# First transfers of a float32 attention and rational FFN kernel: the coefficients on ScalarE's queue, one more pair of words in the fixed order, a bias as a number

## The chip, the cores and the metric

One core of a Trainium2 chip runs the whole program. The metric is device time in microseconds, the median of several executions. TensorE (PE) multiplies and transposes; VectorE (DVE), ScalarE (ACT) and GpSimd (POOL) do the elementwise work; SyncE (SP) issues the transfers between device memory and the on-chip memory. Each engine works through its own instructions in the order of the program and waits on semaphores for the others. TensorE's granted clock has two levels, 2.4 GHz (shown as 1.00) and 1.2 GHz (0.50).

## What is computed

```python
# q, k, v: [8, 8, 576, 64]; p: [8, 8, 32, 64]; w_in: [512, 2048]; w_out: [2048, 512]
def sm_attn(qq, kk, vv):
    s = scale * qq @ kk.T
    e = exp(s - max(s)); return (e / (sum(e) + 1e-9)) @ vv
packed = sm_attn(p, k, v)             # 32 rows of each head
x = sm_attn(q, packed, packed)        # [4608, 512] when the heads are put side by side
h = x @ w_in
P = a[0] + a[1]*h + a[2]*h*h + a[3]*h*h*h
Q = 1 + |b[0]|*|h| + |b[1]|*h*h
out = (P / (Q + 1e-6)) @ w_out
```

q, k, v, p, a and b are float32 here; the two weight matrices come in as 64-bit words (float64), and the kernel turns them into float32 itself. a has four numbers, b has two.

## The kernel before, in words

The batches are bb = 0 to 7. For each, `attention(bb)` makes the packed rows (PPT) and the transposed second softmax (AH, for bb > 0 also its rounded remainder AL). `m_chunk` multiplies the packed rows with a chunk of w_in (M). A unit is one batch, one half x of its 576 rows and one chunk c of 256 of the 2048 hidden columns: 128 units. `hidden` multiplies M with AH into a PSUM bank h, and then runs the rational function: ACT makes |h| (tile U), h squared (sq) and a part of P (Y); POOL adds U and sq; ACT takes the logarithm of the sum, with the bias (1 + 1e-6) * S that stands in a tile `one` of one column, and then the exponential of its negative, back into bank h; DVE does the rest and gives g (tiles gh and gl). `acc_block` multiplies g with w_out into the banks acc, three units later. There are two banks h, two banks acc and two banks at (for everything else).

The first units run in plain float32 and want the weights in words turned early. `load_words` loads one pair of 128-row blocks of words (two transfers of 512 KB), `convert` turns one pair: on ACT a first and a second half (two ACTIVATE of 1024 columns), on DVE two operations of 1024 columns, and an integer addition on DVE or POOL.

`constants` makes what depends on a and b: abS (the coefficients scaled by S), and in the tile `root` a scaled square root of |b[1]|, in a chain of small DVE operations with a logarithm and an exponential on ACT in its middle. ACT then reads some of these numbers into registers (TENSOR_LOAD), and uses them as scales in the units. a and b are loaded by two transfers on SP's queue, with the same value for all 128 partitions (2 KB and 1 KB).

The order of work: every operation outside the set-up goes to `Planner`, which has prices for operations, transfers and signals between engines, tries thirty schedules, and keeps the one that it counts as the shortest; each engine then gets its instructions in that schedule's order. The transfers before `nc.pin()` (the list at line 1004) keep their order and come first on SP. SP waits for a transfer eight places earlier before it issues the next, since eight semaphores go round. Where the plan leaves PE idle for over 180 ns in the first 150 us, `idle` puts in multiplications by a tile of zeros of 96 columns into an open acc bank, here called fillers (line 290): they add nothing to the sums. Each fp32 multiplication of float32 data leaves two records in the trace, so a filler leaves two.

Of the kernel before, what the change touches and what calls it, by code (L numbers as in the profile page):

```python
# [13 lines left out]
F32 = mybir.dt.float32  # L14
# [5 lines left out]
AF = mybir.ActivationFunctionType  # L20
ALU = mybir.AluOpType
AX = mybir.AxisListType
PSUM = bass.MemoryType.PSUM

P = 128
# [4 lines left out]
S = 2.0**-40  # L30


class Planner:
# [8 lines left out]
    TRANSPOSE, F32 = (15, 0.734), (30, 1.62)  # L42
# [19 lines left out]
    SWITCH = 95  # L62
    SLACK = 60, 100, 150, 220, 300
    IN_FLIGHT = 8
    DMA_ISSUE, DMA_START, DMA_END = 420, 1400, 1200

    DMA_RATE = 100.0, 190.0, 370.0
# [27 lines left out]
    def cost(self, engine, name, args, kwargs):  # L95
        if engine == "sync":
            return self.DMA_ISSUE
        fixed, per = self.COST[engine]
        if engine == "tensor":
            if name == "transpose" or args[1].dtype == F32:  # L100
                fixed, per = self.TRANSPOSE if name == "transpose" else self.F32
        aps = [x for x in args if isinstance(x, bass.AP)]
        if engine == "scalar":
            fixed += (aps[-1].space == PSUM) * -42 + ("accum_out" in kwargs) * 93 + ("bias" in kwargs) * 93
            per += 0.1 * any(x.ap[-1][0] == 2 for x in aps[:2])
        if engine == "gpsimd" and len(aps) < 3:
            fixed, per = 135, 0.9
        if engine == "vector" and len(aps) > 2 and any(self.columns(x) == 1 for x in aps[1:]):
            fixed += 60
        if engine == "vector" and name == "tensor_scalar" and len(aps) == 2:  # L110
            per /= 2
        return fixed + per * self.columns(aps[1] if name.startswith("reduce") else aps[0])
# [45 lines left out]
    def edges(self):  # L158
# [32 lines left out]
            edges.append(before)  # L191
        return edges

    def schedule(self, before, after, rank, back=0):

        n = len(rank)
        need = [len(x) for x in before]
        at, start, end = [0.0] * n, [0.0] * n, [0.0] * n
        soon = {e: [] for e in self.ENGINES}
        ready = {e: [] for e in self.ENGINES}  # L200
        free = dict.fromkeys(self.ENGINES, 0.0) if back else dict(self.FIRST)
        port = {"vector": 0.0, "gpsimd": 0.0}
        mode, landed, dma = None, [], 0.0
        for i in range(n):
            if not need[i]:
                heapq.heappush(soon[self.ops[i][0]], (0.0, rank[i], i))
        now = 0.0
        left = n
        while left:
            for e in self.ENGINES:  # L210
                while soon[e] and soon[e][0][0] <= now:
                    heapq.heappush(ready[e], heapq.heappop(soon[e])[1:])
                if free[e] > now or not ready[e]:
                    continue
                if e == "sync" and not back and len(landed) >= self.IN_FLIGHT and landed[-self.IN_FLIGHT] > now:
                    free[e] = landed[-self.IN_FLIGHT]
                    continue
                _, i = heapq.heappop(ready[e])
                left -= 1
                s = now  # L220
                if e == "tensor" and not back and self.modes[i] != mode:
                    s += self.SWITCH
                    mode = self.modes[i]
                if not back and self.shared[i]:
                    s = max(s, port["vector" if e == "gpsimd" else "gpsimd"])
                    port[e] = s + self.costs[i]
                start[i] = s
                end[i] = free[e] = s + self.costs[i]
                if e == "sync":
                    if back:  # L230
                        dma = max(dma, end[i]) + self.transfers[i]
                        end[i] = dma + self.DMA_START + self.DMA_END - self.DMA_ISSUE
                    else:
                        dma = max(dma, s + self.DMA_START) + self.transfers[i]
                        end[i] = dma + self.DMA_END
                        landed.append(end[i])
                for j in after[i]:
                    need[j] -= 1
                    f = self.ops[j][0]
                    way = self.WAY.get((f, e) if back else (e, f), self.PASS)  # L240
                    way += back * (way > 0)
                    at[j] = max(at[j], end[i] + way)
                    if not need[j]:
                        heapq.heappush(soon[f], (at[j], rank[j], j))
            now = min(
                t
                for e in self.ENGINES
                for t in ([free[e]] if ready[e] else [max(soon[e][0][0], free[e])] if soon[e] else [1e12])
            )
        return start, end  # L250
# [74 lines left out]
def attention_rational_ffn(  # L325
# [38 lines left out]

    sb = ctx.enter_context(tc.tile_pool(name="sb", bufs=1))
    ps = ctx.enter_context(tc.tile_pool(name="ps", bufs=1, space=PSUM))
    tc.nc.scalar.preload_act_table_set("natural_log_exp_and_others")
    nc = Planner(tc.nc)


    ident = sb.tile([P, P], F32, name="ident")
    make_identity(tc.nc, ident)
    ab, abS, one, root = (sb.tile([P, n], F32, name=x) for n, x in ((8, "ab"), (7, "abS"), (1, "one"), (5, "root")))
    ab, eps, minus = ab[:, 0:6], ab[:, 6:7], ab[:, 7:8]
    zero = sb.tile([P, 32], F32R, name="zero")
    win = sb.tile([P, NCH, NCC, CF], F32, name="win")
    G = sb.tile([P, NFC, 2 * REM], F32, name="G")
# [25 lines left out]
    def constants():  # L403
        nc.gpsimd.memset(eps, 1e-9)
        nc.gpsimd.memset(minus, -SCALE)
        nc.vector.tensor_scalar(zero, ident[:, 0:32], 0.0, None, ALU.mult)
        nc.sync.dma_start(ab[:, 0:4], a.rearrange("(o n) -> o n", o=1).broadcast_to([P, 4]))
        nc.sync.dma_start(ab[:, 4:6], b.rearrange("(o n) -> o n", o=1).broadcast_to([P, 2]))
        nc.vector.tensor_scalar(abS[:, 0:6], ab, S, None, ALU.mult)
        nc.vector.scalar_tensor_tensor(abS[:, 4:6], abS[:, 4:6], -1.0, abS[:, 4:6], ALU.mult, ALU.max)  # L410
        nc.vector.memset(one, (1.0 + 1e-6) * S)

        m, e, p, r, i = (root[:, n : n + 1] for n in range(5))
        nc.vector.scalar_tensor_tensor(m, ab[:, 5:6], -1.0, ab[:, 5:6], ALU.mult, ALU.max)
        nc.vector.tensor_scalar(m, m, 2.0**-126, None, ALU.max)
        nc.vector.tensor_scalar(e.bitcast(I32), m.bitcast(I32), 23, None, ALU.logical_shift_right)
        nc.vector.tensor_scalar(e.bitcast(I32), e.bitcast(I32), 127, None, ALU.add)
        nc.vector.tensor_scalar(p.bitcast(I32), e.bitcast(I32), 1, 23, ALU.logical_shift_right, ALU.logical_shift_left)
        nc.vector.reciprocal(i, p)
        nc.vector.tensor_scalar(m, m, i, i, ALU.mult, ALU.mult)  # L420
        nc.scalar.activation(r, m, AF.Ln)
        nc.scalar.activation(r, r, AF.Exp, scale=0.5)
        nc.vector.reciprocal(i, r)
        nc.vector.scalar_tensor_tensor(r, m, i, r, ALU.mult, ALU.add)
        nc.vector.tensor_scalar(abS[:, 6:7], r, p, 0.5 * S**0.5, ALU.mult, ALU.mult)
        for i, reg in enumerate((reg_a3, reg_b0, reg_b1, reg_root)):
            nc.scalar.reg_load(reg, abS[0:1, 3 + i : 4 + i].bitcast(I32))
# [458 lines left out]
    def hidden(bb, x, c):  # L886
# [4 lines left out]
        U, V, Y = U_ring.next(), h_ring.next()[:, :, 0:HALF], Y_ring.next()  # L891
        U2 = U2_ring.next()
# [13 lines left out]
        nc.vector.scalar_tensor_tensor(Y, Y, a1, V, ALU.add, ALU.mult)  # L906
        nc.gpsimd.tensor_add(U, U, U2)
        yield
        nc.scalar.activation(U2, U, AF.Ln, bias=one)
        nc.scalar.activation(V, U2, AF.Exp, scale=-1.0)  # L910
        nc.vector.scalar_tensor_tensor(Y, Y, a0, V, ALU.add, ALU.mult)
        nc.vector.scalar_tensor_tensor(V, U, (1.0 + 1e-6) * S, V, ALU.add, ALU.mult)
# [88 lines left out]
        elif i == 1:  # L1001
            nc.sync.dma_start(ov, o)

    for what in ("k0", "k1", "r", "p", "qr", 2, "rv", "v0", "v1", 3, "q0", "q1", 4, 5):
        if isinstance(what, int):
            load_words(what)
        else:
            load(0, what)
    nc.pin()
    constants()  # L1010
    for _ in attention(0):
        pass
# [17 lines left out]
    for bb in range(1, B):  # L1030
        gen = attention(bb)
        at = [u for u in range(2 * UB * bb - 30, 2 * UB * bb - 3) if u not in mt]
# [89 lines left out]
```

## Time and profile before

| | us |
|---|---|
| median of 3 runs | 765.78 (765.69 to 766.87) |
| the profiled execution, its own time | 766.86 |
| its span, first to last instruction | 765.1 |
| PE busy | 737.9 (96%) |
| DVE busy | 656.0 (86%) |
| ACT busy | 619.1 (81%) |
| POOL busy | 467.4 (61%) |

The profile gives, for each engine, when each instruction ran, how long it took, and how long the engine sat idle before it and for whom. The profiled execution took 1.08 us longer than the median, and 1.76 us of its time lie outside the span.

### The profile page before, as it was taken

To read this page: it belongs to the slowest core of one execution; us is meant where nothing else is said; L and a number is where in the kernel's file an instruction comes from. 1 tells how busy PE (TensorE), PEld (TensorE's weight loads), DVE (VectorE), ACT (ScalarE), POOL (GpSimd) and SP (SyncE) were. 2 spreads that over 40 slices of the span, in tenths; PEclk is the share of its full clock that TensorE was granted. 3 is DMA by queue.
4 is the path that set the end of the run, shared out by engine and by line. 5 is a ranking of instruction groups with operands and counts; after the bars stand their busy time and mean duration, and the time that the engine had idled before them with its cause. 6 is when DMAs were issued, how large, how long until landed. Compare 5 with 4: busy or idle time off the path is not lost.

```text
span 765.1 us, 14505 instructions
## 1 busy us (share of the span) xinstructions
PE 737.9 (96%) x5358; PEld 569.2 (74%) x5358; DVE 656.0 (86%) x1050; ACT 619.1 (81%) x1074; POOL 467.4 (61%) x457
## 2 busy tenths in 40 slices
PE   3689999999999999999999999999999999999997
PEld 2455645678788887778788887778788887778886
DVE  2789999898988889998998789998998889988773
ACT  6689986898786888888786888888786887887882
POOL 0026556987685566856685565955685655866672
PEclk8679999999999999999999999999999999999999
DMA  9994650203801128024701119222801016000001
GB/s 253 292 371 129 164 135 0 83 26 50 120 1 56 43 32 126 10 84 55 112 1 57 36 24 126 25 84 32 116 14 56 27 24 83 1 28 1 29 1 41
DMA packets 156630, 56.38 MB, mean 74 GB/s; under 512 B 126864, under 2 KB 145808, under 8 KB 156560
## 3 DMA queue, kind: packets, MB, share of 16 engines
q1 hardware_dynamic: 156560, 55.46, 32.8%
q8 instruction: 42, 0.69, 0.4%
q14 instruction: 28, 0.23, 0.1%
HBM read 46.01 MB, written 9.44 MB: 72 GB/s over the span
## 4 chain that ended last, share of the span: by engine, by line
PE 89%; DMA 4%; ACT 2%; DVE 2%; POOL 1%; SPq 1%; issue 1%; DVEq 0%; POOLq 0%; ACTq 0%
PE acc L293 46%; PE h L293 28%; PE at L293 15%; DMA m<-in_moe_w_in_dram 2%; PE acc L290 1%; DMA pn<-in_p_dram 1%; DVE Y L293 1%; SPq L293 1%; DMA AH<-in_k_dram 1%; ACT sq L293 0%; ACT U L293 0%; POOL U L293 0%; POOL gl L293 0%; ACT h L293 0%; ACT Y L293 0%
## 5 line engine op out<-in xcount | busy, mean ns | idle before, releaser
L293 POOL TENSOR_TENSOR U<-U,sq 128x576 f32<-128x576 f32 x128 | 185.3, 1448 | 140.9 <-ACT sq L293 135.7
L293 DVE SCALAR_TENSOR_TENSOR Y<-Y,abS,h 128x576 f32<-128x576 f32 x256 | 205.7, 804 | 55.0 <-ACT h L293 52.9
L293 PE MATMUL acc<-w,gh 128*128 128x512 f32 x736 | 240.8, 407 | 0.5 <-ACT half L293 0.5
L293 PE MATMUL h<-AH,m 128*128 128x288 f32 x1024 | 195.6, 315 | 1.7 <-DVE AH L293 1.0
L293 PEld LDWEIGHTS h<-AH,m 128*128 128x128 f32 x1024 | 159.2, 189 | 30.8 <-DVE Y L293 7.5
L293 POOL TENSOR_TENSOR gl<-Y,gh 128x512 fp32r<-128x512 f32 x116 | 150.2, 1296 | 31.2 <-POOL G L293 13.5
L293 PEld LDWEIGHTS acc<-w,gh 128*128 128x128 f32 x736 | 133.9, 188 | 45.6 <-issue 16.4
L293 PE MATMUL acc<-w,gl 128*128 128x512 f32 x384 | 150.6, 412 | 0.0
L293 ACT ACTIVATE sq<-U,one 128x576 f32<-128x576 f32 x128 | 101.1, 790 | 34.9 <-POOL U L293 34.7
L293 ACT ACTIVATE U<-h 128x576 f32<-128x576 f32 x128 | 83.3, 651 | 40.3 <-PE h L293 39.6
L293 DVE TENSOR_TENSOR Y<-Y,h 128x576 f32<-128x576 f32 x128 | 95.3, 745 | 16.0 <-ACT Y L293 15.7
L293 ACT ACTIVATE h<-sq 128x576 f32<-128x576 f32 x128 | 84.8, 663 | 21.6 <-DVE Y L293 20.0
L293 PE MATMUL h<-AL,m 128*128 128x288 f32 x448 | 97.0, 296 | 0.0
L293 ACT ACTIVATE Y<-h,abS 128x576 f32<-128x576 f32 x128 | 96.5, 754 | 0.0
L293 DVE SCALAR_TENSOR_TENSOR h<-U,h 128x576 f32<-128x576 f32 x128 | 95.9, 749 | 0.0
L293 PEld LDWEIGHTS acc<-w,gl 128*128 128x128 f32 x384 | 71.8, 188 | 22.9 <-issue 10.2
L293 DVE SCALAR_TENSOR_TENSOR Y<-h,Y 128x576 f32<-128x576 f32 x116 | 87.0, 750 | 1.9
L293 ACT CAST gh<-Y 128x512 fp32r<-128x512 f32 x116 | 73.0, 629 | 14.8 <-DVE Y L293 10.1
L293 ACT ACTIVATE sq<-h 128x576 f32<-128x576 f32 x128 | 83.5, 653 | 0.0
L293 PE MATMUL acc<-half,gh 128*128 128x512 f32 x240 | 78.2, 409 | 0.2 <-ACT gh L293 0.2
L293 PEld LDWEIGHTS h<-AL,m 128*128 128x128 f32 x448 | 71.9, 188 | 2.0 <-issue 1.4
L293 PEld LDWEIGHTS acc<-half,gh 128*128 128x128 f32 x240 | 43.9, 188 | 13.5 <-issue 5.1
(145 smaller groups left out, 904.3 us busy)
## 6 DMA issues: line engine op xcount, KB each, us to landing
w<-in_moe_w_out_dram SPq DMA_DIRECT2D x16, 512.0 KB, 5.1
out_dram<-half SPq DMA_DIRECT2D x15, 512.0 KB, 3.0
nat<-in_k_dram SPq DMA_DIRECT2D x48, 144.0 KB, 4.3
nat<-in_q_dram SPq DMA_DIRECT2D x48, 144.0 KB, 4.4
nat<-in_v_dram SPq DMA_DIRECT2D x24, 256.0 KB, 3.3
m<-in_moe_w_in_dram SPq DMA_DIRECT2D x10, 512.0 KB, 8.9
w<-in_moe_w_in_dram SPq DMA_DIRECT2D x6, 512.0 KB, 8.2
nat<-in_k_dram SPq DMA_DIRECT2D x4, 512.0 KB, 7.1
```

The source lines that it names most:

```text
L290: getattr(self.nc.tensor, name)(*args, **kwargs)
L293: getattr(getattr(self.nc, engine), name)(*args, **kwargs)
```

## The change

Three things. The two transfers of a and b leave SP's queue and `constants`; they become the first two instructions of ScalarE, issued on ScalarE's own queue ahead of its table load. The planner no longer orders them; in their place it counts what reads `ab` as ready 4.5 us after the start (`LANDED`, `ready`). The list of fixed first transfers gets a sixth pair of words. The bias of the logarithm is given as a number instead of the tile `one`, whose memset falls away, and the planner's price takes its 93 ns for a bias only where the bias is a tile.

```diff
+    LANDED = 4500.0
-            fixed += (...) + ("bias" in kwargs) * 93
+            fixed += (...) + isinstance(kwargs.get("bias"), bass.AP) * 93
...
+    def ready(self, calls):
+        return self.LANDED * any(isinstance(x, bass.AP) and x.tensor.name == "ab" for _, args, _ in calls for x in args)
...
-                heapq.heappush(soon[self.ops[i][0]], (0.0, rank[i], i))
+                at[i] = 0.0 if back else self.ready(self.ops[i][1])
+                heapq.heappush(soon[self.ops[i][0]], (at[i], rank[i], i))
...
+    tc.nc.scalar.dma_start(ab[:, 0:4], a.rearrange("(o n) -> o n", o=1).broadcast_to([P, 4]))
+    tc.nc.scalar.dma_start(ab[:, 4:6], b.rearrange("(o n) -> o n", o=1).broadcast_to([P, 2]))
     tc.nc.scalar.preload_act_table_set("natural_log_exp_and_others")
...
-        nc.sync.dma_start(ab[:, 0:4], a.rearrange("(o n) -> o n", o=1).broadcast_to([P, 4]))
-        nc.sync.dma_start(ab[:, 4:6], b.rearrange("(o n) -> o n", o=1).broadcast_to([P, 2]))
-        nc.vector.memset(one, (1.0 + 1e-6) * S)
...
-        nc.scalar.activation(U2, U, AF.Ln, bias=one)
+        nc.scalar.activation(U2, U, AF.Ln, bias=(1.0 + 1e-6) * S)
...
-    for what in ("k0", "k1", "r", "p", "qr", 2, "rv", "v0", "v1", 3, "q0", "q1", 4, 5):
+    for what in ("k0", "k1", "r", "p", "qr", 2, "rv", "v0", "v1", 3, "q0", "q1", 4, 5, 6):
```

Since the planner plans anew, the order of all engines changes beyond the first 25 us. Three places are shown. In the names, the first number belongs to the buffer and the last counts the tiles; kx, AH, at, acc, h, m, gh are as above, and w and half hold words or weights.

The first is the start of ACT, before:

```order
L1118 UNCONDITIONAL_BRANCH
L367 ACT_TABLE_LOAD
L293 COPY kx0_1_87<-at0_1_91 128x512
```

after:

```order
L1123 UNCONDITIONAL_BRANCH
L375 DMA ab_61<-in_moe_a_dram 128x4
L376 DMA ab_61<-in_moe_b_dram 128x2
L377 ACT_TABLE_LOAD
L299 TENSOR_LOAD abS_62 x2
L299 ACTIVATE root_63<-root_63 128x1 x2
L299 TENSOR_LOAD abS_62
L299 COPY kx0_1_89<-at0_1_91 128x512
```

The chain of the constants with its register loads now stands ahead of ACT's first copy; before, it stood some thirty-five instructions later, among the copies of chunk 1.

The second is ACT from the first units' three operations to the copies of batch 1's transposes, before:

```order
L293 ACTIVATE Y1_2_139<-h1_2_138,abS_68 128x576
L293 ACTIVATE sq0_1_129<-U0_1_126,one_69 128x576
L293 COPY m1_7_134<-at0_21_147 128x256
L293 ACTIVATE h0_1_127<-sq0_1_129 128x2x288
L293 COPY m1_7_134<-at1_22_148 128x256
L293 ACTIVATE sq1_2_140<-U1_2_137,one_69 128x576
L293 COPY kx0_2_141<-at0_23_154 128x512
L293 COPY kx0_2_141<-at1_24_155 128x512
L293 ACTIVATE h1_2_138<-sq1_2_140 128x2x288
L293 COPY kx0_2_141<-at0_25_159 128x256
```

after:

```order
L299 ACTIVATE Y1_2_140<-h1_2_139,abS_62 128x576
L299 COPY m1_7_135<-at0_21_148 128x256
L299 COPY m1_7_135<-at1_22_149 128x256
L299 ACTIVATE w2_5_121<-w2_5_121 128x1024
L299 ACTIVATE sq0_1_130<-U0_1_127 128x576
L299 ACTIVATE sq1_2_141<-U1_2_138 128x576
L299 ACTIVATE h0_1_128<-sq0_1_130 128x2x288
L299 COPY kx0_2_142<-at0_23_155 128x512
L299 COPY kx0_2_142<-at1_24_156 128x512
L299 ACTIVATE h1_2_139<-sq1_2_141 128x2x288
L299 COPY kx0_2_142<-at0_25_160 128x256
```

A half of a pair of words and both logarithms now stand ahead of the copies of the transposes at_23 and at_24.

The third is PE where batch 1's packed rows wait for DVE, before:

```order
L293 MATMUL at0_35_195<-rv0_2_110,small_74 32x64
L290 MATMUL acc1_14_167<-half0_1_157,zero_71 32x96 x14
L293 MATMUL at1_34_194<-ident_62,small_74 128x128
L290 MATMUL acc1_14_167<-half0_1_157,zero_71 32x96 x2
L293 MATMUL h0_7_190<-AH0_3_114,m1_7_134 128x288 x4
```

after:

```order
L299 MATMUL at0_35_196<-rv0_2_112,small_75 32x64
L299 MATMUL acc0_13_167<-half1_2_179,gl1_2_182 128x512 x2
L299 MATMUL acc1_14_168<-half0_1_158,gh1_2_172 128x512 x2
L299 MATMUL acc1_14_168<-half1_2_179,gl1_2_182 128x512 x2
L299 MATMUL at1_34_195<-ident_67,small_75 128x128
```

Six multiplications of the units' sums, done earlier before, now stand where 14 fillers stood. In the whole program there are 41 fillers before and 11 after (one of them 256 columns wide).

## Rows read from the trace of the kernel before

**Rows 1.** The page: the span.

```profile
span 765.1 us, 14505 instructions
```

**Rows 2.** Stretches: from:to, length, busy us by engine, PEclk, DMA share, GB/s.

```profile
0.00:38.00 38.00, 20.12 (x261) 13.75 (x261) 20.28 (x52) 23.79 (x44) 1.12 (x10) 0.79 0.93 273
38.00:53.00 15.00, 11.62 (x55) 8.10 (x56) 13.24 (x24) 11.19 (x23) 3.04 (x3) 0.73 1.04 365
53.00:100.00 47.00, 47.00 (x367) 28.14 (x366) 43.43 (x75) 46.80 (x79) 25.85 (x14) 1.00 0.65 180
100.00:168.00 68.00, 67.12 (x380) 39.98 (x378) 63.47 (x100) 55.87 (x88) 51.42 (x43) 1.00 0.17 44
168.00:761.00 593.00, 592.06 (x4298) 479.20 (x4298) 515.10 (x804) 481.42 (x843) 385.94 (x390) 1.00 0.27 48
```

**Rows 3.** Stretches, fillers of line 290 alone: PE, PEld busy, PEclk, DMA, GB/s.

```profile
53.00:100.00 47.00, 6.24 (x62) 4.95 (x62) 1.00 0.65 180
100.00:168.00 68.00, 1.84 (x20) 1.62 (x20) 1.00 0.17 44
```

**Rows 4.** PE in order of time: start, us, operation, count [idle before, released by].

```profile
20.89 1.92 PE L293 MATMUL acc<-w,kx 128*32 128x64 f32 x60 [0.97 <-DMA w<-in_v_dram]
...
38.25 4.21 PE L293 MATMUL h<-AH,m 128*128 128x288 f32 x8 [0.96 <-DVE AH L293]
...
48.98 1.98 PE L293 MATMUL at<-ident,nat 128*128 128x128 f32 x8 [2.98 <-ACT m L293]
50.99 1.12 PE L293 MATMUL at<-ident,AH 128*128 128x128 f32 x4
...
52.33 1.28 PE L293 MATMUL acc<-w,gh 128*128 128x512 f32 x2
53.45 2.10 PE L293 MATMUL h<-AH,m 128*128 128x288 f32 x8
```

**Rows 5.** ACT in order of time.

```profile
5.95 0.58 ACT L293 COPY kx<-at 128x512 f32<-128x512 f32 x1 [3.93 <-PE at L293]
...
23.66 1.15 ACT L293 ACTIVATE m<-m 128x1024 f32<-128x1024 f32 x1 [4.28 <-DMA m<-in_moe_w_in_dram]
...
42.23 1.19 ACT L293 ACTIVATE w<-w 128x1024 f32<-128x1024 f32 x1 [3.60 <-DVE abS L293]
43.31 1.06 ACT L293 COPY kx<-at 128x512 f32<-128x512 f32 x2
44.47 0.65 ACT L293 ACTIVATE U<-h 128x576 f32<-128x576 f32 x1
...
47.85 0.81 ACT L293 ACTIVATE sq<-U,one 128x576 f32<-128x576 f32 x1
48.52 0.41 ACT L293 COPY m<-at 128x256 f32<-128x256 f32 x1
48.77 0.71 ACT L293 ACTIVATE h<-sq 128x576 f32<-128x576 f32 x1
49.36 0.43 ACT L293 COPY m<-at 128x256 f32<-128x256 f32 x1
```

**Rows 6.** DVE in order of time: the second half of AH.

```profile
41.71 0.77 DVE L293 STREAM_TRANSPOSE AH<-kx 128x576 f32<-128x576 f32 x1
```

**Rows 7.** Stretches around batch 1's transposes, columns as in rows 2.

```profile
48.00:52.00 4.00, 2.87 (x13) 2.15 (x14) 3.78 (x6) 3.94 (x9) 0.86 (x1) 0.68 1.06 371
52.00:56.00 4.00, 4.00 (x29) 2.37 (x27) 3.46 (x6) 3.94 (x6) 0.00 (x0) 0.89 1.04 394
```

**Rows 8.** Transfers: operation, count, KB each, median us to landing.

```profile
pn<-in_p_dram SPq DMA_DIRECT2D x8, 16.0 KB, 4.7
ab<-in_moe_b_dram SPq DMA_DIRECT2D x1, 1.0 KB, 10.4
ab<-in_moe_a_dram SPq DMA_DIRECT2D x1, 2.0 KB, 9.3
```

**Rows 9.** The tile root: operations, count: ns min/median/max, first and last start.

```profile
L293 DVE TENSOR_SCALAR root<-root x5: 141/146/267, 34.5 to 37.2; 128x1 int32<-128x1 int32 x3, 128x1 f32<-128x1 f32 x2
```

More of the change, by code (lines that the diff above doesn't have):

```diff
@@ L103, in cost @@
         if engine == "scalar":
-            fixed += (aps[-1].space == PSUM) * -42 + ("accum_out" in kwargs) * 93 + ("bias" in kwargs) * 93
+            fixed += (aps[-1].space == PSUM) * -42 + ("accum_out" in kwargs) * 93 + isinstance(kwargs.get("bias"), bass.AP) * 93
             per += 0.1 * any(x.ap[-1][0] == 2 for x in aps[:2])
@@ L366, in attention_rational_ffn @@
     ps = ctx.enter_context(tc.tile_pool(name="ps", bufs=1, space=PSUM))
+    ab, abS, root = (sb.tile([P, n], F32, name=x) for n, x in ((8, "ab"), (7, "abS"), (5, "root")))
+    ab, eps, minus = ab[:, 0:6], ab[:, 6:7], ab[:, 7:8]
+    tc.nc.scalar.dma_start(ab[:, 0:4], a.rearrange("(o n) -> o n", o=1).broadcast_to([P, 4]))
+    tc.nc.scalar.dma_start(ab[:, 4:6], b.rearrange("(o n) -> o n", o=1).broadcast_to([P, 2]))
     tc.nc.scalar.preload_act_table_set("natural_log_exp_and_others")
@@ L372, in attention_rational_ffn @@
     make_identity(tc.nc, ident)
-    ab, abS, one, root = (sb.tile([P, n], F32, name=x) for n, x in ((8, "ab"), (7, "abS"), (1, "one"), (5, "root")))
-    ab, eps, minus = ab[:, 0:6], ab[:, 6:7], ab[:, 7:8]
     zero = sb.tile([P, 32], F32R, name="zero")
```

## The prediction, made before the changed kernel was run

> **What bounds the kernel now.** The first view is the table of stretches [rows 2], read for which engine is full where, and after it the single engines in order of time. Up to 38 us nothing is full for long: the 16 DMA engines are 93% busy, and PE waits for landings, as for v at 20.89 us [rows 4]. From 38 to 53 us the clock is at its lower level for part of the time (mean 0.73) and PE, DVE and ACT wait for one another. From 53 us on PE is the bound: it idles 0.88 us up to 168 us, and 0.94 us in the 593 us after that. But up to 168 us not all of its work is needed: 82 records of fillers, two to a filler, take 6.24 + 1.84 = 8.08 us [rows 3], 0.197 us a filler. There DVE (106.90 of 115 us) and, up to 100 us, ACT (46.80 of 47 us) are nearly full as well, so the fillers mark where PE waited for them. After 168 us a saving on any engine but PE is worth nothing. So the question is how much earlier PE gets through the first 168 us.
>
> **The change, part by part.**
>
> *The bias.* The logarithm goes from 0.67 us (47.85 to 48.52) towards the 0.59 us that the exponential takes between starts (48.77 to 49.36) [rows 5]: 0.08 us, times 128 some 10 us of ACT. Some 120 of the units run after 100 us, where ACT is idle for 124 us and PE doesn't wait for it: nothing. Up to 100 us it is about eight, 0.6 us of ACT; I count it in the fillers' term, since both are the same relief.
>
> *The coefficients at the start.* ACT's first copy (5.95 us) now stands behind the chain of the constants, and that behind the landing of a and b. The chain is some seven DVE steps of 0.146 us [rows 9], two small ACT steps, three more DVE steps and a register load; with a signal between each I estimate 3.3 us. What lies behind: the copies, the first attention, the words. The cover: ACT is idle 4.28 us before 23.66 us [rows 5], and PE waited 0.97 us for v [rows 4]; and ACT itself waited 3.93 us for PE before the first copy, and the next copies also come as fast as PE makes them. So I estimate that the copies can be some 2.3 us late for nothing. That holds for a landing up to 5.95 + 2.3 - 3.3 = 4.9 us from the span's start. The trace shows no small transfer with an empty queue. The nearest rows are 4.7 us for 16 KB, and 9.3 and 10.4 us for a and b themselves, behind SP's backlog [rows 8]. Issued at about 1 us, these give landings at 5.7 and 10.3 us, so a loss of 0.8 or of 5.4 us; below, a loss of nothing. I take 0.2 us, since here only the first transfer of k is in front of them.
>
> The rows put a and b behind a backlog of SP's. The Trainium skill (DMA: Bandwidth & Descriptors, "Issuing engines are not separate DMA queues") says that transfers issued from several engines run on the same 16 DMA engines and interleave, and that it saves only the time to issue. By it the second queue is no faster path, but interleaving would let a and b pass the megabytes of k, and the loss would be 0 instead of 0.2 us; no row here shows two queues side by side.
>
> *The sixth pair.* 1 MB of words takes the place of a and b on SP, ahead of batch 1's k. At 273 to 365 GB/s [rows 2] that is 2.7 to 3.8 us later for what follows. Batch 1's transposes of k come, in the order of before, only after the 38.25 us group of PE. In the new order they come just before it. So I cost it at nothing, with a bound of 1 us if k is late. In return ACT turns this pair in the 3.60 us that it waited for abS, up to 42.23 us [rows 5]. A copy of batch 1 still may not start until DVE has made the second half of AH (41.71 + 0.77 = 42.48 us) [rows 6], as the two share the buffer kx; so ACT gains work done ahead, not an earlier unit.
>
> *Early loss, 38 to 57 us.* From that point I follow ACT in the new order by the old times. Two copies of 0.53 and a half pair of 1.08 us (both from 42.23 to 44.37) [rows 5] from 42.9 us on: the first unit's operations start at 45.05 instead of 44.47 us. Six of these take 47.85 - 44.47 = 3.38 us, to 48.43. Two chunk copies of 0.25 us: 48.93, and PE makes the transposes at_23 and at_24 at the same 48.95 us as before. But then ACT does a half pair (1.08), two logarithms (0.59 each) and an exponential (0.59) before it copies them, so the copies end at 52.3 and 52.85. PE goes on with the next transposes at 52.5 instead of 50.99 us [rows 4], with batch 1's scores at 54.4, and with the first sum (acc) at 55.5 instead of 52.33. Up to 55.5 us the old order had done the sum's first multiplication (1.1 us) and the second pair of units' first half (2.1 us), the new one instead the scores (0.7): 2.5 us behind. In the old trace the clock fell to its lower level after the idle stretch before 48.98 and rose inside 52 to 56 us (means 0.68 and 0.89) [rows 7], when PE had been busy for close to 4 us. With more idle time in between it should rise later, near 57 us: another 0.6 us or more. I take 3.1 us of loss on PE, with bounds of 1.0 (ACT is not held up) and 4.5 us (all of it cold).
>
> *Fillers.* 30 of 41 go: 30 x 0.197 = 5.9 us that PE doesn't spend. What replaces the largest group, 14 of them where batch 1's packed rows wait for DVE, is work: six multiplications of the sums. That is the early loss coming back. But where the inputs are later than the plan, idle time takes the place of fillers. Call these new waits w: between 0 and 5.9 us. DVE says that w isn't 0: it is 93% busy up to 168 us and has its 8.1 us of idle time for this, of which the early loss takes some. I take 1.0 us, near the lower end, by PE's 0.88 us of idle time in the same stretch, which shows that the old plan's gaps were met.
>
> *After 168 us.* The order changes, PE's work doesn't: 0, with bounds of half a microsecond either way by the 0.94 us of idle time.
>
> Sum: -5.9 + 3.1 + 0.2 + 1.0 = -1.6 us. The profiled execution took 766.86 us, 1.76 of it outside its span of 765.1 [rows 1], which I leave as they are; it would take 765.3; its 1.08 us over the median are not the kernel's, so the median goes from 765.78 to 764.2.
>
> **Rivals.**
> 1. *The relief is real and the early loss isn't.* ACT starts 42.9 us with one pair more turned than before; if the copies aren't behind the half pair by a whole microsecond, the loss is 1.0 and w near 0: -4.9 at the most, -4.3 us with 0.6 of waits: 761.5.
> 2. *DVE bounds it.* The constants leave DVE's full stretch, but otherwise its work is the same, and 93% of the time is spoken for. Then w = 2.6 us, and the fillers were only a picture of a wait: 765.8. PE's unbroken run after each filler speaks against it, ACT's full 53 to 100 us for it.
> 3. *Slower: fillers turn into idle time.* The early loss stays because the second and third pair of units come some 3 us later from ACT, and DVE gets them too late to give it back. It decides at w = 2.6 us (no gain), and at w = 4.1 us the kernel is slower by 0.2%. At w = 5 us: 768.2.
> 4. *a and b land late.* As in the old trace, after 9.3 us: 5.4 us lost, 769.4. It decides at a landing near 4.9 us; for it speaks that k's transfers are issued at the same time, against it that the backlog of old is not there yet. The interleaving of the page named above lowers its chance; I give it 0.06.
> 5. *The change does not do what it says*, as the number for a bias might be put into a tile again: then the order shown would still hold, and only some tenths of ACT's time go: inside the forecast.
>
> **How the numbers follow.** 0.2% (1.53 us) is about what a measurement of this kernel can tell from no change. The forecast has 0.42, and as it lies on that line, 0.22 of it is faster and 0.20 the same. Rival 1 has 0.22 (faster), rival 2 0.18 (same), rival 3 0.12 and rival 4 0.06 (slower). So faster 0.44, same 0.38, slower 0.18. Range: from 760.8 (rival 1 with no waits) to 767.6, which leaves out most of rivals 3 and 4 and little else.
>
> **What would show it.** In the profile after: ACT's first copy at 7 to 8.3 us and PE's v product still near 20.9 us (the start is free); no 3.6 us wait of ACT near 42 us; the first acc multiplication near 55.5 us; fillers of about 2 us; PE idle by 1 to 3 us between 57 and 168 us; and after that the same 593 us. A first copy past 9 us, or an acc multiplication at 52 us, or idle time over 4 us would prove a step wrong, and so would a change of more than 1 us behind 168 us.

## The result, and the profile after

The changed kernel takes 774.38 us (median of 4 runs, 773.47 to 775.44), the kernel before 766.33 us beside it: a ratio of 1.0095, with an interval of 1.0076 to 1.0114. It is slower by 0.95%, where 0.2% faster was forecast, and lies outside the range. The profiled execution took 774.68 us; its span is 7.8 us longer than that of [rows 1].

```profile
span 772.9 us, 14401 instructions
```

The same stretches as in [rows 2], with the same columns; the last is given twice, first as long as it was before:

```profile
0.00:38.00 38.00, 20.81 (x245) 15.49 (x245) 19.41 (x50) 21.14 (x40) 1.06 (x9) 1.00 0.92 294
38.00:53.00 15.00, 10.39 (x64) 6.80 (x64) 12.74 (x21) 12.65 (x23) 5.49 (x4) 0.74 0.88 281
53.00:100.00 47.00, 43.77 (x277) 25.36 (x278) 41.65 (x73) 41.60 (x73) 21.45 (x12) 0.90 0.54 168
100.00:168.00 68.00, 66.40 (x400) 39.41 (x399) 63.36 (x98) 56.90 (x94) 52.14 (x41) 1.00 0.26 59
168.00:761.00 593.00, 589.07 (x4281) 473.69 (x4280) 522.80 (x808) 475.05 (x848) 385.53 (x390) 1.00 0.26 48
168.00:769.00 601.00, 596.83 (x4314) 479.78 (x4312) 523.64 (x810) 476.17 (x849) 388.06 (x392) 1.00 0.26 47
```

The trace of this execution holds no clock record before 31 us, so the mean clock of 1.00 in its first stretch says nothing; in e13, a run with the same order told below, it is 0.82. PE was idle for 0.94 us of the 593 us behind 168 us; now it is 3.93 us, and DVE is busy for 522.80 instead of 515.10 us of them. From 53 to 168 us PE's idle time goes from 0.88 to 4.83 us. The fillers, which answer to [rows 3], are down from 8.08 to 2.49 us:

```profile
53.00:100.00 47.00, 1.20 (x10) 0.77 (x10) 0.90 0.54 168
100.00:168.00 68.00, 1.29 (x11) 0.91 (x11) 1.00 0.26 59
```

The start and the place of batch 1's transposes, in order of time (columns as in [rows 4]): first ACT, then the second half of AH on DVE, then PE.

```profile
10.71 0.58 ACT L299 COPY kx<-at 128x512 f32<-128x512 f32 x1 [1.08 <-PE at L299]
...
45.37 1.07 ACT L299 COPY kx<-at 128x512 f32<-128x512 f32 x2 [2.25 <-DVE AH L299]
...
51.30 1.22 ACT L299 ACTIVATE w<-w 128x1024 f32<-128x1024 f32 x1
52.37 1.29 ACT L299 ACTIVATE sq<-U 128x576 f32<-128x576 f32 x2
53.53 0.68 ACT L299 ACTIVATE h<-sq 128x576 f32<-128x576 f32 x1
```

```profile
44.49 0.77 DVE L299 STREAM_TRANSPOSE AH<-kx 128x576 f32<-128x576 f32 x1
```

```profile
20.85 1.40 PE L299 MATMUL acc<-w,kx 128*32 128x64 f32 x44 [0.67 <-DMA w<-in_v_dram]
...
51.25 1.19 PE L299 MATMUL at<-ident,nat 128*128 128x128 f32 x8 [2.59 <-ACT m L299]
54.77 1.12 PE L299 MATMUL at<-ident,AH 128*128 128x128 f32 x4 [2.33 <-ACT kx L299]
55.68 0.63 PE L299 MATMUL at<-ident,pn 128*128 128x128 f32 x2
56.78 1.32 PE L299 MATMUL at<-kx,small 64*32 64x256 f32 x24 [0.46 <-ACT small L299]
58.03 2.07 PE L299 MATMUL acc<-w,gh 128*128 128x512 f32 x2
```

The first copy comes at 10.71 instead of 5.95 us, the second half of AH 2.78 us late (44.49 against 41.71), and the first multiplication into acc 5.70 us late (58.03 against 52.33). PE waits 2.33 us for the copies of its transposes, which stand behind the half pair and the two logarithms. From 52 us the clock is at its lower level until 60 us is past; before, its mean from 53 to 100 us was 1.00 [rows 2] (columns as in [rows 7]):

```profile
52.00:56.00 4.00, 1.67 (x10) 1.25 (x7) 2.26 (x4) 3.83 (x8) 0.90 (x1) 0.51 1.07 333
56.00:60.00 4.00, 3.54 (x29) 1.59 (x28) 4.00 (x9) 3.95 (x6) 0.00 (x0) 0.50 1.06 381
60.00:64.00 4.00, 4.00 (x13) 2.95 (x12) 3.33 (x6) 2.06 (x5) 0.00 (x0) 0.71 0.93 248
```

PE's waits behind 168 us (whom it waited for: us in total, times, longest):

```profile
PE h L299 <- DVE Y L299: 3.2, 7, 0.9
```

In the kernel before:

```profile
PE h L293 <- DVE Y L293: 0.2, 1, 0.2
```

A bank h comes free when DVE has made the unit's last Y from it; so DVE is late there.

How far the kernels are apart along the way is read from the start of ACT's logarithms, one for each unit, with the units counted from 0; here against the kernel before, in us (e13 and e14 are runs told below):

| unit | before, start | changed | e13 | e14 |
|---|---|---|---|---|
| 16 | 151.29 | +7.41 | +7.74 | -1.26 |
| 32 | 241.50 | +2.89 | +2.31 | -4.96 |
| 64 | 414.45 | +5.63 | +3.03 | -4.93 |
| 96 | 588.53 | +7.23 | +3.10 | -5.87 |
| 127 | 747.23 | +7.99 | +3.22 | -6.09 |

Up to some 200 us the orders differ in what else they have done by then; from unit 32 to the last the changed kernel loses another 5.1 us, little by little. Its order differs from that of before there as well, so single rows can be off by a microsecond or two; e13 below, which has the same order, gives the same 5.1 us.

### The profile page after: what moved, and what is told of

Its sections match the earlier page's. It is cut to its first block, busy times and chain, and to the rows that moved or that the text cites. A ratio compares the mean times of both kernels' runs of the same rounds, so it can differ in the third digit from the quotient of the medians.

```text
span 772.9 us, 14401 instructions
## 1 busy us (share of the span) xinstructions
PE 738.2 (96%) x5297; PEld 566.9 (73%) x5297; DVE 661.3 (86%) x1049; ACT 608.5 (79%) x1074; POOL 468.2 (61%) x457
## 4 chain that ended last, share of the span: by engine, by line
PE 64%; DVE 20%; ACT 10%; issue 4%; POOL 1%; DMA 1%; SPq 0%; DVEq 0%; ACTq 0%; POOLq 0%
PE acc L299 33%; PE h L299 20%; PE at L299 11%; DVE Y L299 10%; DVE small L299 3%; DVE kx L299 3%; DVE h L299 2%; ACT sq L299 2%; ACT h L299 1%; ACT U L299 1%; ACT Y L299 1%; DVE m L299 1%; ACT m L299 1%; DMA nat<-in_k_dram 1%; ACT kx L299 1%
## 5 line engine op out<-in xcount | busy, mean ns | idle before, releaser
L299 ACT ACTIVATE sq<-U 128x576 f32<-128x576 f32 x128 | 88.7, 694 | 31.5 <-POOL U L299 31.4
L299 PE MATMUL acc<-half,gh 128*128 128x512 f32 x240 | 80.0, 411 | 0.0
```

The costliest lines, as they stand in the source:

```text
L299: getattr(getattr(self.nc, engine), name)(*args, **kwargs)
```

## Experiments: the start, the queue, the number

**The planner's count made to work (e1).** The tile's name is `ab_61`, not `ab`, so `ready` gave 0 for everything: the plan took a and b as there from the start. That is why the chain of the constants came ahead of ACT's first copy.

```diff
-    LANDED = 4500.0
+    LANDED = 10000.0
-        ... x.tensor.name == "ab" ...
+        ... x.tensor.name.startswith("ab_") ...
```

> The changed kernel, with the planner's count of the coefficients made to work: `ready` looks for the tensor name `ab`, the tile's name is `ab_61`, so the rule never held, and the plan took a and b as there at 0. Here it looks for names that begin with `ab_`, with 10 us. Only the first 26 instructions of ACT, 28 of DVE and 12 of POOL stand otherwise; the chain of the constants comes behind ACT's first copies. Theory (the late first copy, 10.71 instead of 5.95 us, costs the 2.5 to 2.8 us by which AH is late, and the new order of work behind it costs the other 5): first copy near 6 to 8 us, second half of AH near 42 us, 771.7 us (771.0 to 772.4). Rival A (the whole loss hangs on the late start, since the order behind it only fits the plan's times): 767.5 us or less. Rival B (the start is covered and the order alone costs): 773.4 us or more.

773.62 us, ratio 1.0098 (1.0070 to 1.0126): rival B. The first copy came at 7.52 us, and the first multiplication into acc at 55.75 us, 2.3 us earlier than in the changed kernel:

```profile
55.75 2.07 PE L299 MATMUL acc<-w,gh 128*128 128x512 f32 x2
```

But the ratio is that of the changed kernel. The late start is real and costs little or nothing at the end. (The theory, 771.0 to 772.4 us, had given the start some 2.5 us.)

**The coefficients not read (e2).**

```diff
+    unread = sb.tile([P, 6], F32, name="unread")
+    tc.nc.vector.memset(ab, 1.0)
-    tc.nc.scalar.dma_start(ab[:, 0:4], ...)
+    tc.nc.scalar.dma_start(unread[:, 0:4], ...)
...
```

> The changed kernel in its own order, with the chain of the constants ahead of ACT's first copy, but the transfers of a and b go into a tile that nobody reads, and the coefficients are all set to 1: the wait for the landing is taken away, and the transfers remain. Left out: the given coefficients. Theory (the wait for the landing is what holds the first copy): the chain runs from about 1 us and ends near 5 us, the first copy starts near 6 to 8 us, 771.7 us, as in the run with the chain behind the copies. Rival A: 767.5 us or less. Rival C (the chain itself, with its register loads, holds the copies as much as the landing): between 773 and 774.4 us.

773.72 us, ratio 1.0092 (1.0063 to 1.0121). The first copy came at 7.68 us, so the landing held it and not the chain. The time stays, as in e1: it is the time that rival C named, but not for its reason. In this execution the early copies didn't even help as far as 58 us: the first multiplication into acc came at 58.09 us (changed kernel: 58.03), since ACT now waited for words of w_in that the changed kernel's ACT took at 46.33 us without a wait:

```profile
46.41 1.18 ACT L299 ACTIVATE w<-w 128x1024 f32<-128x1024 f32 x1 [1.44 <-DMA w<-in_moe_w_in_dram]
```

**The queue alone, in the old order (e3, again as e18, and e16).** e3 and e18 are the same kernel:

```diff
+    tc.nc.scalar.dma_start(ab[:, 0:4], ...)      # ahead of the table load
+    tc.nc.scalar.dma_start(ab[:, 4:6], ...)
...
+                if engine == "sync" and args[0].tensor.name.startswith("ab_"):
+                    continue
```

> The kernel before in its own order to the last instruction, but for the two transfers of a and b, which go first on ACT's queue and no longer on SP's. The chain of the constants stays where it was, near 34 us. Theory (the queue as such costs nothing, the chain ahead of the copies does): 766.3 us, 765.5 to 767.1. Rival D (the two transfers on the second queue hold up the first transfers of k and p, which landed some 2 us later in the changed kernel): 767.5 to 769 us with the first copy past 7 us.

> The kernel before in its own order, a and b first on ACT's queue: the same kernel as the first run of the queue alone (768.92 us, ratio 1.002 to 1.0051). If the second queue costs: 768 to 769.5 us again. If that was chance: 766 to 767.5 us, and the queue is worth nothing.

First 768.92 us, ratio 1.0035 (1.0020 to 1.0051); again, with more runs, 768.64 us beside 767.24, ratio 1.0009 (0.9995 to 1.0022). In e16 the two transfers are issued behind ACT's sixth copy:

```diff
+                if engine == "scalar" and name == "copy" and self.late:
+                    copies += 1
+                    while copies == 6 and self.late:
+                        ...   # the two dma_start of ScalarE
```

> The kernel before in its own order, a and b on ACT's queue, but issued behind ACT's sixth copy, near 10 us. Theory (what costs in the run with the queue alone is that two small transfers stand beside the first transfers of k and p, which then land later): 766.3 us, first copy near 5.95 us. Rival L (leaving SP's queue is what costs, since later transfers of SP then come earlier and take other turns of the eight semaphores): 768 to 769 us.

768.09 us, ratio 1.0010 (0.9995 to 1.0026), with the first copy at 6.04 us; that doesn't tell the theory from rival L. So the second queue delays the first transfers (first copy at 7.69 us in e3), but what it costs at the end lies between nothing and some 0.5%: the intervals of the two runs of one kernel share no more than 1.0020 to 1.0022, and their profiled executions don't agree either: in e3's the units are not late against the kernel before, in e18's they are 2 us late from 80 us on. It stays open.

**The number alone, in the old order (e4).**

```diff
-        nc.scalar.activation(U2, U, AF.Ln, bias=one)
+        nc.scalar.activation(U2, U, AF.Ln, bias=(1.0 + 1e-6) * S)
```

> The kernel before in its own order to the last instruction, with the logarithm's bias given as a number (the price and the memset of the tile stay). Theory (ACT is not the bound): Ln from 0.67 to 0.59 us between starts, 766.3 us, 765.7 to 766.8. Rival E (ACT's relief of 0.08 us a unit reaches PE up to 100 us): 765.2 us or less.

765.64 us, ratio 0.9979 (0.9962 to 0.9996). Over the whole run (line, operation, count | busy us, mean ns | idle before) the logarithm goes from 790 to 696 ns:

```profile
L293 ACT ACTIVATE sq<-U 128x576 f32<-128x576 f32 x128 | 89.0, 696 | 35.1 <-POOL U L293 35.0
```

(before:)

```profile
L293 ACT ACTIVATE sq<-U,one 128x576 f32<-128x576 f32 x128 | 101.1, 790 | 34.9 <-POOL U L293 34.7
```

A small gain, and its interval nearly reaches 1. In the profiled execution the units are 0.40 us late at 100 us and 0.70 us early at the end, so it falls behind 100 us, where the prediction had "nothing"; that was too strict, by some 0.2%.

## Experiments: the order of work

**Each part alone, planned anew (e5, e6, e7), and one price (e8).** e5 has the number, its lower price and no tile `one`; e6 has only the sixth pair; e7 only a and b on ACT's queue, with the dead count. e8 is the kernel before but for this:

```diff
-    COST = {"vector": (70, 1.04), ...
+    COST = {"vector": (71, 1.04), ...
```

> The kernel before with the bias as a number and its price alone, planned anew; a and b stay on SP, five pairs stay fixed. The four runs so far say: the later start costs little (putting the constants back gave 0.8 of some 8 us), the queue alone 2 us, the number alone nothing or a small gain; so the loss lies in the new order of work. Theory (no part of the change is at fault: any new plan brings waits of its own, an early one near 50 us and small ones of PE for DVE's Y in the whole run, since the planner tells plans apart that differ by less than it misses the chip's times by): a change of 1 to 6 us against the kernel before, with waits of PE for Y after 168 us of 1 us or more. Rival F (the sixth pair is at fault: its half stands ahead of the copies of batch 1): here no loss, 764.5 to 767 us. Rival G (the lower price of the logarithm packs ACT and DVE too tightly): a loss of 3 us or more here, and none in the other three.

> The kernel before with the sixth pair in the fixed order alone, planned anew. In ACT's new order the half pair stands ahead of the copies of batch 1's transposes, as in the changed kernel. Theory (any new plan brings waits of its own): a change of 1 to 6 us. Rival F (the sixth pair is at fault): 771 us or more, first acc multiplication past 54.5 us. Rival G: 766 us.

> The kernel before with a and b on ACT's queue (and the planner's rule that never holds) alone, planned anew. The chain of the constants stands ahead of ACT's first copy; the copies of batch 1 stand before the second logarithm and behind no half pair. Theory (any new plan brings waits of its own): a change of 1 to 6 us. Rival F: the 2 us of the queue at most, 767 to 769 us. Rival G: the same as F.

> The kernel before with one price of the planner changed by 1 ns: 71 instead of 70 ns as the fixed part of a VectorE operation. No instruction differs but in its place: from ACT's fortieth instruction on all engines have another order. Theory (any new plan brings waits of its own): a difference of 1 us or more to the kernel before, PE's waits after 168 us unlike those of before. Rivals F and G: within 1 us, 765.5 to 767.5.

e5: 771.49 us, ratio 1.0059 (1.0043 to 1.0076). e6: 766.11, 0.9992 (0.9977 to 1.0008). e7: 775.19, 1.0121 (1.0104 to 1.0138). e8: 771.79, 1.0074 (1.0057 to 1.0091). e8 settles it: 1 ns in one price, which changes no instruction but the fillers, only places, costs 0.74%, with PE waiting 5.1 us for Y behind 168 us. Rival F falls with e6. Rival G falls with e7 and e8, which have no lower price and lose more. The order that the planner happens to draw decides, and the order of before was a good one. The theory's 1 to 6 us were too narrow: e6 didn't change, and e7 lost 8.7 us.

**The half pair behind the copies (e9).** One instruction of ACT moved in the changed kernel's order:

```diff
+        a, b = order.index(half), order.index(copy)      # w2_5's first half; the copy of at_25
+        order[a : b + 1] = order[a + 1 : b + 1] + [half]
```

> The changed kernel in its own order but for one instruction of ACT: the half pair w2_5 (1.08 us), which stands ahead of both logarithms and of the copies of batch 1's transposes at_23 to at_25, now stands behind these copies. Theory (the early stall is real at its place, but most of an early delay is given back or lost again later, as the run with the constants behind the copies showed): PE's wait for kx near 54.8 us falls from 2.33 to some 1.2 us, the first acc multiplication comes 1 us earlier than 58.03, and the end moves by 0 to 0.8 us, 773.5 to 774.4 us. Rival H (the prediction's own step: what is lost here is lost at the end, with the clock on top): 772 to 773.3 us.

775.27 us, ratio 1.0098 (1.0071 to 1.0125): no gain. PE began these transposes at 53.56 instead of 54.77 us, but it was 1.13 us ahead before the moved instruction already (50.12 against 51.25 us for the group before them), so the move itself gave next to nothing: PE's wait there is 2.35 us, as it was 2.33, and not the 1.2 expected. The half pair had stood for the most part in a time in which ACT would have waited for POOL:

```profile
51.77 0.68 ACT L307 ACTIVATE sq<-U 128x576 f32<-128x576 f32 x1 [0.68 <-POOL U L307]
```

Then PE waited 1.31 instead of 0.46 us for ACT's `small`, and the third unit's logarithm came 0.5 us earlier.

**The changed kernel with another draw (e11), and without its first part (e12).** e11 is the changed kernel with the 71 of e8. e12 has a and b on SP as before, with the sixth pair, the number and the lower price that the changed kernel counts for it.

> The changed kernel with one price of the planner changed by 1 ns (71 instead of 70 for the fixed part of a VectorE operation); in its new order the half pairs w2_5 stand behind the copies of batch 1's transposes. Theory (a plan is a draw, the three edits do not decide it): 766 to 778 us, away from the 774.4 of the changed kernel by 1 us or more. Rival I (the three edits together cost 8 us in whatever order): 773.5 to 775.5 us.

> The changed kernel with its first part undone: a and b on SP's queue as before, the sixth pair and the number with its price kept, planned anew. Theory (a plan is a draw): anything from 765 to 773 us. Rival J (the queue and the chain in front, with what they do to the order, are the loss): 766 us or less. Rival G (the lower price of the logarithm): 770 us or more, with the half pair behind or ahead of the copies.

e11: 768.65 us, ratio 1.0021 (1.0009 to 1.0034). e12: 768.03, ratio 1.0018 (1.0007 to 1.0028). The same three edits cost 0.2% in one draw and 0.95% in another; rival I falls. Rival J isn't confirmed either: e12 didn't come to 766 us, and e11, which has the queue, costs no more than e12. Rival G falls once more with e12.

**The sixth pair's order with the number (e10).** e6 with the bias of e4, its price kept, so that the order of e6 stays.

> The run with the sixth pair alone, in its own order to the last instruction, with the number as the logarithm's bias (its old price kept, so that the plan stays). Theory (an order that came out well is kept, and the number gives 0.08 us a unit where PE waits for ACT or DVE, some 1 us in all as in the order of before): 765.0 us, 764 to 766, faster than the kernel before by 0.1 to 0.3%. Rival (the gain of the number in the order of before was chance): 766.1 us, as without it.

765.33 us, ratio 0.9963 (0.9944 to 0.9982): faster than both kernels, though its interval overlaps that of e6.

## Experiments: what in an order costs the time

In the changed kernel's trace DVE and POOL stand like this around 493 us (in order of time):

```profile
492.98 1.33 DVE L299 TENSOR_SCALAR small<-small,ab 128x18 f32<-128x18 f32 x1
494.22 0.75 DVE L299 SCALAR_TENSOR_TENSOR h<-U,h 128x576 f32<-128x576 f32 x1
```

```profile
492.84 1.43 POOL L299 TENSOR_TENSOR U<-U,sq 128x576 f32<-128x576 f32 x1 [1.61 <-ACT sq L299]
494.22 1.30 POOL L299 TENSOR_TENSOR gl<-Y,gh 128x512 fp32r<-128x512 f32 x1
```

The DVE operation has 18 columns and takes 0.23 us at 213.34 us, where POOL is idle. Here it takes 1.33 us, and ends (494.30) as POOL's operation does (494.27). DVE stays behind, and 7 us later PE waits:

```profile
501.44 0.77 PE L299 MATMUL h<-AH,m 128*128 128x288 f32 x4 [0.89 <-DVE Y L299]
```

In e8 the same stands at 312.28 (1.10 us, POOL's from 312.06 for 1.29) and again at 315.18 (1.03 us, POOL's from 314.89 for 1.30), and PE then waits 1.35 us at 318.28. There are sixteen such operations, two a batch: they add 1e-9 to the sums of the second softmax. In the changed kernel ten of them take 0.62 to 1.33 us, in the kernel before five:

```profile
L299 DVE TENSOR_SCALAR small<-small,ab 128x18 f32<-128x18 f32 x16 | 10.3, 646 | 0.0
```

(before:)

```profile
L293 DVE TENSOR_SCALAR small<-small,ab 128x18 f32<-128x18 f32 x16 | 6.9, 434 | 0.0
```

Over both kernels, 17 of the 32 take 0.38 us or more (12 in the changed kernel, 5 before). Each of the 17 begins while POOL is at work and ends 0.03 us after POOL's operation; the other 15 take 0.22 to 0.27 us. The reciprocal of the same 18 columns, which follows, isn't held, though in each kernel 6 or 7 of its 16 stand beside a POOL operation from start to end (all take 0.22 to 0.26 us):

```profile
L299 DVE RECIPROCAL small<-small 128x18 f32<-128x18 f32 x16 | 4.0, 247 | 0.0
```

The busy time hides the wait, since DVE counts as busy while it is held. The Trainium skill (SBUF — State Buffer, "Who interferes with whom") says that DVE and GpSimd share a pair of ports as an exclusive lock, that a `tensor_scalar` is among the operations that can take it, and that who comes second is blocked until the first is done. The ends above agree, in all 17; no run moves POOL's operation away, so the lock itself is read from these times and not tested. The planner's rule for shared operations (`shares`) doesn't count this one: it has one wide input, and a tile as its number.

**The sixteen operations left out (e13 to e15).** In the order of the changed kernel, of e10, and of before; all other instructions keep their places. A sum has at least the 1 of its own maximum in it, and 1e-9 doesn't change that in float32.

```diff
+                if name == "tensor_scalar" and getattr(args[0], "shape", (0, 0))[-1] == 18 and args[2].tensor.name.startswith("ab_"):
+                    continue
```

> The changed kernel in its own order, without 16 DVE operations: those that add 1e-9 to the 18 sums of the second softmax (two a batch). In the trace of the changed kernel 12 of the small operations of DVE take 0.62 to 2.37 us in place of 0.27, and end when an operation of POOL ends; some 1 to 8 us later PE waits for Y. Theory (these make DVE late, and DVE's lateness is what PE waits for): PE's waits for Y fall from 4.7 to below 2.5 us, 771 to 772.5 us. Rival K (DVE's order alone, with the operations of m ahead of Y, is what makes Y late): waits as before, 773.5 to 774.4 us. DVE's busy time falls by 8 to 10 us in either case.

> The run with the sixth pair and the number in the order of the sixth pair alone (765.33 us), without the same 16 operations of DVE. Theory: PE's waits for Y of 1.3 us go for the most part, 764.2 us, 763.3 to 765. Rival K: 765.3 us as without.

> The kernel before in its own order, without the same 16 operations. PE waits for Y only 0.2 us in it, so there is little to win: theory and rival both 765.5 to 766.5 us; a gain of over 1 us would show that DVE's lateness costs PE in ways that are not shown as waits for Y.

e13: 768.53 us, ratio 1.0028 (1.0015 to 1.0040). The changed kernel gets back 0.0067 of its 0.0095, some 5.1 us, from 16 operations of 10.3 us in all, on an engine that isn't the bound. The stretch behind 168 us is again like that of before:

```profile
168.00:761.00 593.00, 592.15 (x4303) 478.40 (x4302) 516.19 (x797) 476.08 (x849) 388.42 (x392) 1.00 0.26 48
```

```profile
PE h L301 <- DVE Y L301: 0.3, 1, 0.3
```

and in the table above the lag goes from 2.31 us at unit 32 to 3.22 at the end. PE's 5297 multiplications stand in the same order in both, so they can be compared one by one: at 168 us e13 is 0.33 us later than the changed kernel, at the end 4.77 us earlier. Of these 5.1 us, 4.4 come at nine places, at each of which the changed kernel's PE waits before a multiplication into h, and e13's doesn't. (Each place costs some 0.15 us more than the wait that it shows, so PE's idle time of 3.93 us is less than the loss.) The theory (771 to 772.5 us) holds, by more than it asked for; rival K falls.

e15: 766.23 us, ratio 0.9996 (0.9985 to 1.0008): in the order of before the same operations cost nothing that can be told from 0.1%. e13 takes out the short ones with the long ones; that the long ones are what costs is argued from e15 and from the places of PE's waits, and no run tests it by itself. e14: 761.32 us, ratio 0.9933 (0.9916 to 0.9950): the fastest of all, below its forecast of 763.3 to 765, and faster than e10 by 0.3% (the intervals just meet).

```profile
span 758.8 us, 14365 instructions
```

**What is left: the early stall (e17).** e13 with the count of e1 and the move of e9.

> The changed kernel in its own order without the 16 operations of DVE (768.5 us), and with both early delays taken away: the constants behind ACT's first copies (the planner's count at 10 us) and the half pair w2_5 behind the copies of batch 1's transposes. Theory (what is left of the loss is the early stall, which two small repairs can shorten by 1 to 3 us): PE's transposes at_23 near 49 us, first acc multiplication before 56 us, 766 to 767.5 us. Rival M (the early stall is given back by itself, as half pair and late start alone showed): 768.3 to 769 us.

768.25 us, ratio 1.0011 (1.0000 to 1.0023); its interval and that of e13 overlap, and the 766 to 767.5 us of the theory weren't reached. Its profiled execution doesn't show the repair: ACT came to the words of w_in 2.93 us before they landed, and PE then waited 5.80 us, until 51.44, for a copy of m:

```profile
46.58 1.14 ACT L309 ACTIVATE w<-w 128x1024 f32<-128x1024 f32 x1 [2.93 <-DMA w<-in_moe_w_in_dram]
```

e2's waited until 46.41 and e13's until 47.39 us for the same words, while in e1's ACT had them at 44.04. So in some executions the words are the next limit behind the late start and take back what an earlier start gives. The early stall's rest is between 0.1 and 0.3% of the time, and how much of that the two repairs take isn't settled.

## Why the prediction was wrong

- **"After 168 us: 0" is the step that failed.** It measured some 5 us: e13 takes 4.8 us off the span (772.9 to 768.1) and 5.1 us off the time behind 168 us, and PE's idle time there is again like that of before. The argument was that PE's work is the same and its idle time small. But the 0.94 us of idle time belonged to the old order, not to the work: DVE is 87% busy there, and e13 shows that sixteen small operations of its, twelve of them behind 168 us, are worth 5 us in these places and nothing in those of before (e15). The bound of half a microsecond was read from the very trace that the change throws away. No rival had this place.
- **The start.** The first copy was to come at 7 to 8.3 us, and past 9 us the step was wrong; it came at 10.71. The landing of a and b was taken at 4.9 us; they took 5.0 and 6.5 us from issues at 0.74 and 1.21, so 7.7 us:

```profile
ab<-in_moe_a_dram ACTq DMA_DIRECT2D x1, 2.0 KB, 5.0
ab<-in_moe_b_dram ACTq DMA_DIRECT2D x1, 1.0 KB, 6.5
```

  By the step's own rule that is 7.7 - 4.9 = 2.8 us, and AH was 2.78 us late. The rule was right and its input wrong; that the two figures agree to 0.02 us is luck, since from the landing to the copy it took 3.0 us and not the estimated 3.3, and the 2.3 us of cover were never measured. The page of the Trainium skill that was weighed there (DMA: Bandwidth & Descriptors, "Issuing engines are not separate DMA queues") was right that they would interleave with SP's transfers (5.0 and 6.5 us here, behind SP's backlog 9.3 and 10.4 us [rows 8]), but not for nothing: k's first copies moved too, by 1.7 us in e3. At the end the start was worth next to nothing (e1, e2).
- **The early loss** was followed rightly: at_23 and at_24 wait behind the half pair and the logarithms (2.33 us), and with the start taken out the first acc multiplication comes at 55.75 us (e1), where 55.5 was forecast. Two things were not on that path: the half pair alone cost next to nothing, as POOL would have held ACT there for most of its time (e9), and the landing of the words of w_in can hold ACT at 46 to 47 us (e2, e13, e17). The clock rose past 60 us, not near 57: from 52 to 64 us PE is busy 1.67, 3.54 and 4.00 us of each four at 0.51, 0.50 and 0.71. The 0.6 us or more that was allowed for it was probably too little; what the clock alone cost no run tells.
- **The fillers** went from 8.08 to 2.49 us, 5.6 of the 5.9 us. The new waits w: outside the early stall PE is idle some 2.6 us up to 168 us, 1.7 more than before, where 1.0 was taken. With that, the first 168 us lose some 2 to 3 us (e13: ratio 1.0028, span 768.1 against [rows 1]) in place of the gain of 1.6.
- **Rivals.** Rival 4's mechanism came (a late landing), at a price that the rest covered. Rival 5 came in a place that wasn't looked at: the count in `ready` never held. Rival 3 gave the right sign by the wrong place.
- **The bias** was right on PE's side but for some 0.2% (e4), and **the sixth pair** costs nothing by itself (e6).

The chain of waits tells the same as the failed step: its share on PE was 89% before and is 64% now, with 20% on DVE (before, then changed).

```profile
PE 89%; DMA 4%; ACT 2%; DVE 2%; POOL 1%; SPq 1%; issue 1%; DVEq 0%; POOLq 0%; ACTq 0%
PE 64%; DVE 20%; ACT 10%; issue 4%; POOL 1%; DMA 1%; SPq 0%; DVEq 0%; ACTq 0%; POOLq 0%
```

## What to carry to other kernels

Where a program searches for the order of work, any edit is also a new draw of that order: measure the edit in the old order first, and give the new draw its own spread, here 0 to 1.2% from edits worth 0.2%. A nearly full bound engine doesn't say that its feeders have slack: look for small operations of theirs that are long now and then, and for what ends when they end. A rule that looks something up by name should be seen to hold once.

## What the runs showed of the hardware

An 18-column DVE operation of 0.23 us took 1.44 us beside a POOL operation (e10, at 128.61 us: it ended at 130.05, POOL's at 130.02), and a DVE reciprocal of the same 18 columns was never held. Two transfers of 1 and 2 KB at the head of ACT's queue held back SP's first ones: the two of `AH<-in_k` landed after 9.9 us in e3 and 9.8 in e18 (median), against 6.9 in the kernel before. And one kernel's executions can part early and stay apart: e3's profiled execution took 766.57 us, e18's 768.97. At 48.82 and 49.63 us they begin batch 1's transposes 0.81 us apart, PE shows no other wait up to 80 us, and yet the units are 2.1 to 2.4 us apart from there to the end; the mean granted clock from 53 to 100 us was 1.00 in the one and 0.97 in the other:

```profile
53.00:100.00 47.00, 47.00 (x367) 28.10 (x366) 43.76 (x75) 46.26 (x78) 26.35 (x14) 1.00 0.65 182
```

```profile
53.00:100.00 47.00, 46.83 (x363) 27.96 (x363) 43.03 (x73) 45.76 (x77) 23.69 (x13) 0.97 0.62 171
```

(e3 first, then e18.)
